# Moving one weight block's decode behind a second set of peaks, and spreading four pairs' sums by transposes

## The chip, the cores and the metric

The kernel runs on one core of one Trainium2 chip. The metric is the device time of one execution in microseconds (us). The engines are named as the profile names them: PE is TensorE's matmul, PEld its weight load, DVE is VectorE, ACT is ScalarE, POOL is GpSimd and SP is SyncE, which issues most of the DMAs. A small letter q behind an engine (SPq, ACTq) is that engine's queue of DMA issues.

## What is computed

Attention with a window of 128 keys and 4 sink keys, and a feed-forward network on what comes out of it. The shapes are B=4, H=8, S=768 and D=64 for q, k and v, and 3072 tokens with 512 to 2048 to 512 features for the network; `w_in` and `w_out` come as 64-bit floats.

```python
keep = is_sink | in_window                      # S x S
scores = np.where(keep, scores, -1000000000.0)
scores = scores - np.max(scores, axis=-1, keepdims=True)
a = np.exp(scores)
a = a / (np.sum(a, axis=-1, keepdims=True) + 1e-09)
attn_out = np.matmul(a, v)

x = attn_out.transpose(0, 2, 1, 3).reshape(B * S, H * D)
h = x @ w_in
g = np.where(h >= 1, h, np.where(h <= -1, 0.0, (h + 1) ** 2 / 4))
return g @ w_out
```

## The kernel before, in words

The 3072 tokens are cut into eight chunks of 384, a chunk being one batch entry and one half of its sequence. For each chunk the attention of eight heads fills `xn`, 512 features by 384 tokens, `split` (L617) turns that into two halves `x`, a rounded part and the rest, and the network runs on them: `stage1` (L582, its matmuls at L588) and `stage2` (L602, matmuls at L607), three matmuls for each product. The attention of chunk c+1 is spread over the network of chunk c, so PE always has network matmuls to do, except ahead of the first chunk: there `first_pairs` (L523) does the attention of chunk 0 with nothing to cover it.

The first sixteen heads (chunks 0 and 1) are computed in plain float32, two heads at a time, in eight **pairs** m = 0 to 7. For one pair:

- `pair_load` (L408) fetches keys and queries (DMAs at L415 and L416), `pair_values` (L419) the values `vq` (L423, L424);
- `pair_scores` (L431) does two score matmuls for each of three row tiles (L441), into `o_ps`, `h_ps` or `ps_a`; DVE takes the row maxima, called **peaks** below (L452), and ACT the exponentials with their row sums (L457);
- `pair_sums` (L460) adds 1e-9 (L464) and takes the reciprocals (L465): six numbers for each partition;
- `early_transp` (L468) transposes the weights of the two heads on PE (L474, L476), and ACT copies them to `pt` (L477, L478, L480);
- `pair_r` (L498) spreads the reciprocals: six float32 matmuls (L505), each of 64 by 128 outputs, whose left operand is one column of reciprocals broadcast to 64 columns and whose right operand is the identity. ACT copies the 128 by 384 result to `xn` (L507);
- `pair_av` (L482) multiplies weights and values (L493), and DVE multiplies `xn` by the product (L496).

Pairs 0 to 3 and the scores of pair 4 are in `first_pairs`. Pairs 5 to 7 and what is left of pair 4 are written as steps with weights (`pair_steps`, L509) and spread over the network of chunk 0: `spread` (L637) takes attention steps so that their summed weights keep pace with those of the network's steps, so a step's weight sets where PE does it.

The weights come in sixteen blocks of 1 MB, `w_in` and `w_out` in turn, and must be **decoded** from 64-bit words before use. One decode is four steps (L164 on): shift on DVE (L170), sign on DVE (L176), tail on DVE (L179) with a copy on ACT (L180), and the rest on DVE (L183); each of the DVE steps is on 128 by 1024 elements. Blocks 0 to 3 are decoded inside `first_pairs`, a step here and there between the pairs' peaks; there `d[0]` to `d[3]` are the four steps, in `m`'s turn. The other twelve are spread over chunk 0's network. The block's DMA (L205) is issued by SP for blocks 0 to 3 and by ACT for the others.

What sets the order: PE works in program order. In `first_pairs`, DVE and ACT instructions that go through `queue` (L64) are also kept in program order among themselves. Every other instruction of DVE, ACT, POOL and SP is placed by the compiler's scheduler, which plans each engine's queue from a model of the whole program; an engine then works through its queue strictly in that order. Loads for the first head of chunk 2, whose attention follows the pairs (`load`, L262 and L264, and `values`, L324, with its cast to `vsx` at L326 on ACT and the subtract at L327 on POOL), have no need of anything before them and are placed inside `first_pairs`' stretch. The tile `vs_r` has one buffer, so each L324 waits until POOL's L327 of the one before is done.

Of the kernel before, what the change touches and what calls it, by code (L numbers as in the profile page):

```python
# [8 lines left out]
F32 = mybir.dt.float32  # L9
F32R = mybir.dt.float32r  # L10
# [5 lines left out]
B, H, S, D = 4, 8, 768, 64  # L16
DM, DFF = 512, 2048
P = 128
NT = S // P
CT = 3  # L20
# [29 lines left out]
def attn_ffn(ctx, tc, qk, qkp, vx, vs, par, w_in, w_out, out):  # L50
    nc = tc.nc
# [12 lines left out]
    def queue(i, on=True):  # L64
        if on:
            e = i.ins.engine
            if e in queued:
                tc.add_manual_dep(i.ins, queued[e].name, mybir.DependencyInfo(
                    mybir.DependencyClass.NoSync, mybir.DependencyReason.DATA), reason="queue")
            queued[e] = i.ins  # L70
        return i

    ident = const.tile([P, P], F32, name="ident")
# [176 lines left out]
    att = fast.enter_context(tc.tile_pool(name="att", bufs=2))  # L250
    fast.enter_context(tc.manual_schedule(engines={mybir.EngineType.PE}))
    st = {}
# [155 lines left out]
    def pair_load(m):  # L408

        b, h, _ = units[2 * m]  # L410
        T = CT * P
        W = CT * KB - NSINK
        q_s = att.tile([P, T], F32R, name="q_h").bitcast(F32)
        k_s = att.tile([P, P + CT * KB], F32R, name="k_s").bitcast(F32)[:, :W]
        loaded.append(nc.sync.dma_start(k_s, qkp[b, h // 2, :, T:T + W]).ins)  # L415
        nc.sync.dma_start(q_s, qkp[b, h // 2, :, 0:T])  # L416
        st["qk", m] = q_s, k_s

    def pair_values(m):  # L419
        v_s = vq[m % 2]  # L420
        for a in range(2):
            b, h, _ = units[2 * m + a]
            nc.sync.dma_start(v_s[:, :CT, a], vx[b, h, :, :CT])  # L423
            nc.sync.dma_start(v_s[:NSINK, CT, a], vx[b, h, :NSINK, 0])  # L424
# [35 lines left out]
    def pair_sums(m):  # L460
        on = m < H // 2
        stat = st.pop(("sum", m))
        r = stat[:, :, CT:2 * CT]
        queue(nc.vector.tensor_scalar(r, stat[:, :, 0:CT], 1.0e-9, None, op0=ALU.add), on)  # L464
        queue(nc.vector.reciprocal(r, r), on)  # L465
        st["r", m] = r

    def early_transp(u, part):  # L468

        p, pt = early_p(u), pt0[u % 2]  # L470
        on = u < H
        ps = ps_a.tile([P, 512], F32, name="ps_a")
        for n, (i, c) in enumerate((((0, KB), (1, 0), (1, KB)), ((2, 0), (2, KB)))[part]):
            nc.tensor.transpose(ps[:, n * P:(n + 1) * P], p[:, i, c:c + P], ident)  # L474
        if part:
            nc.tensor.transpose(ps[:NSINK, 2 * P:CT * P], p[:, CT - 1, P:KB], ident)  # L476
            queue(nc.scalar.copy(pt[:, CT * P:5 * P], ps[:, :2 * P]), on)  # L477
            queue(nc.scalar.copy(spn[u % 2][:NSINK], ps[:NSINK, 2 * P:CT * P]), on)  # L478
        else:
            queue(nc.scalar.copy(pt[:, :CT * P], ps[:, :CT * P]), on)  # L480

    def pair_av(m):  # L482

        T = CT * P
        v_s = vq[m % 2]
        ps = ps_a.tile([P, 512], F32, name="ps_a")

        terms = [(2, 4, 1, 2), (0, 0, 2, 0), (1, 2, 2, 1), None]
        for n, t in enumerate(terms):
            for a in range(2):  # L490
                k, s0, ns, i = t or (CT, 0, 1, CT - 1)
                rhs = pt0[a][:, s0 * P:(s0 + ns) * P] if t else spn[a]
                nc.tensor.matmul(ps[a * D:a * D + D, i * P:(i + ns) * P], lhsT=v_s[:, k, a], rhs=rhs,  # L493
                                 start=(n == 0), stop=(n == len(terms) - 1))
        x = xn[:, units[2 * m][1] // 2, :]
        return lambda: queue(nc.vector.tensor_tensor(x, ps[:, :T], x, op=ALU.mult), m < H // 2)  # L496

    def pair_r(m):  # L498

        T = CT * P  # L500
        ps = ps_a.tile([P, 512], F32, name="ps_a")
        r = st.pop(("r", m))
        for i in range(CT):
            for a in range(2):
                nc.tensor.matmul(ps[a * D:a * D + D, i * P:(i + 1) * P], lhsT=r[:, a, i:i + 1].broadcast_to([P, D]),  # L505
                                 rhs=ident, start=True, stop=True)
        queue(nc.scalar.copy(xn[:, units[2 * m][1] // 2, :], ps[:, :T]), m < H // 2)  # L507

    def pair_steps(m):  # L509

        a, b = 2 * m - 2, 2 * m - 1
        sc = [(0.45, lambda i=i: pair_scores(m, i)) for i in range(CT)] if m < NATIVE // 2 else [(0.0, lambda: None)] * CT
        steps = [(0.0, lambda: pair_load(m + 1))] if m + 1 < NATIVE // 2 else []
        if m < NATIVE // 2:
            steps.append((0.0, lambda: pair_values(m)))
        tp = [(0.35, lambda u=u, i=i: early_transp(u, i)) for u in (a, b) for i in range(2)]
        pv = [(0.65, lambda: pair_r(m - 1)), (1.2, lambda: pair_av(m - 1)())]
        dg = [(0.0, lambda: pair_sums(m))] if m < NATIVE // 2 else []
        if m % (H // 2) == 0:
            return steps + tp[:3] + sc[:1] + tp[3:] + pv[:1] + sc[1:2] + pv[1:] + sc[2:] + dg  # L520
        return steps + tp[:1] + sc[:1] + tp[1:] + sc[1:2] + pv + sc[2:] + dg

    def first_pairs():  # L523
        pair_load(0)
        pair_load(1)
        pair_values(0)
        d = None
        for m in range(H // 2 + 1):
            if m:
                pair_load(m + 1)  # L530
                pair_values(m)
                for u in (2 * m - 2, 2 * m - 1):
                    for part in range(2):
                        early_transp(u, part)
            if m == H // 2:
                pair_r(m - 1)
                d[2]()
                pair_av(m - 1)()
            pair_scores(m, 0)
            pair_scores(m, 1)  # L540
            if 0 < m < H // 2:
                d[2]()
            pair_scores(m, 2)
            if m:
                d[3]()
            if 0 < m < H // 2:
                pair_r(m - 1)
            pair_sums(m)
            if m < H // 2:
                wsteps[m][0]()  # L550
                d = wsteps[m][1]()
                d[0]()
                if m:
                    pair_av(m - 1)()
                d[1]()


    chunks = [(b, t) for t in (0, CT) for b in range(B)]
# [101 lines left out]
    wsteps = [weights(n) for n in range(NP)]  # L660
# [33 lines left out]
    ps = ps_a.tile([P, 512], F32, name="ps_a")  # L694
# [56 lines left out]
    with tc.If(other_v > 0):  # L751
        with tc.tile_pool(name="gen", bufs=1) as gen:

            for n in range(2 * NJ):
# [3 lines left out]
                m = gen.tile([P, DM], F32, name="m")  # L758
# [3 lines left out]
            for t0 in (0, CT):  # L762
                keep = gen.tile([P, CT, S], F32, name="keep")
                kidx = gen.tile([P, S], I32, name="kidx")
                r = gen.tile([P, S], F32, name="r")
                for i in range(CT):
                    m = keep[:, i]
# [54 lines left out]
```

## Time and profile before

| what | value |
|---|---|
| runs | 706.54 us, median of 3 (705.92 to 707.37) |
| profiled execution, own time | 705.98 us |
| its span in the profile | 704.3 us |
| mean granted TensorE clock | 0.994 of full speed |
| busy: PE, DVE, ACT, POOL | 681.5, 510.3, 489.5, 278.8 us |
| instructions | 12263 |

The span runs from the first instruction's start to the last one's end; 1.7 us of the execution's time lie around it. Busy times include time in which an instruction stands in the engine's pipeline, so two neighbours can overlap by some tenths of a microsecond. In the timeline a row gives the start, the time of one or of several merged instructions, the engine, the line of the kernel, and the operation with the tile written, an arrow and the tiles read; in square brackets stands how long the engine was idle before, and what ended that.

### The profile page before, as it was taken

How to read it: one execution, taken by the hardware profiler on the slowest of the kernel's cores; microseconds unless marked ns; L12 is line 12 of the kernel's file. 1: busy time of each engine (PE TensorE's matmuls, PEld its weight loads, DVE VectorE, ACT ScalarE, POOL GpSimd, SP SyncE). 2: the span in 40 equal slices, each digit the busy share in tenths (PEclk: the TensorE clock that was granted, in tenths of full speed). 3: DMA queues.
4: the chain of work that ended last, by engine and by line, in shares of the span. 5: the costliest groups of instructions: out<-in, count | busy, mean ns of one | idle time of the engine just before them, and what ended most of it. 6: DMA issues, size and time to landing. Idle time of an engine off the chain costs nothing.

```text
span 704.3 us, 12263 instructions
## 1 busy us (share of the span) xinstructions
PE 681.5 (97%) x3889; PEld 604.6 (86%) x3889; DVE 510.3 (72%) x1405; ACT 489.5 (70%) x1241; POOL 278.8 (40%) x470
## 2 busy tenths in 40 slices
PE   5899998999999999999999999999999999999996
PEld 3567877899999999989889999899899999989995
DVE  7888998887776877688777878878787877642221
ACT  4886667687778868777787877777776876554332
POOL 3003344744443445355554455635544444300000
PEclk9899999999999999999999999999999999999999
DMA  7864533132244344254333443434322310001001
GB/s 232 291 216 156 190 99 135 49 107 60 63 148 124 102 127 129 68 174 128 92 113 105 147 130 124 126 118 133 122 59 62 102 50 22 3 1 45 1 1 49
DMA packets 45441, 73.98 MB, mean 105 GB/s; under 512 B 10744, under 2 KB 30008, under 8 KB 45368
## 3 DMA queue, kind: packets, MB, share of 16 engines
q1 hardware_dynamic: 42104, 60.53, 28.2%
q10 hardware_dynamic: 3264, 12.58, 4.8%
q8 instruction: 33, 0.54, 0.3%
q14 instruction: 40, 0.33, 0.1%
HBM read 66.80 MB, written 6.29 MB: 104 GB/s over the span
## 4 chain that ended last, share of the span: by engine, by line
PE 79%; DVE 9%; DMA 3%; ACT 3%; POOL 3%; issue 2%; SPq 0%; ACTq 0%; POOLq 0%; DVEq 0%
PE h_ps L588 33%; PE o_ps L607 32%; PE ps_a L283 4%; PE ps_a L390 4%; PE ps_a L344 2%; DVE bits L176 2%; DVE bits L179 1%; DMA w<-w_in 1%; POOL q_l L269 1%; PE ps_a L474 1%; DVE w L183 1%; DVE bits L170 1%; PE ps_a L493 1%; DVE p L304 1%; DVE g L597 1%
## 5 line engine op out<-in xcount | busy, mean ns | idle before, releaser
L588 PE MATMUL h_ps<-x,wi 128*128 128x384 f32 x1536 | 310.2, 340 | 0.0
L588 PEld LDWEIGHTS h_ps<-x,wi 128*128 128x128 f32 x1536 | 262.2, 188 | 8.7 <-issue 1.5
L607 PE MATMUL o_ps<-w,gh 128*128 128x512 f32 x768 | 244.0, 398 | 0.0
L607 PE MATMUL o_ps<-w,gl 128*128 128x512 f32 x384 | 151.1, 393 | 0.4 <-POOL gl L599 0.4
L607 PEld LDWEIGHTS o_ps<-w,gh 128*128 128x128 f32 x768 | 134.3, 188 | 16.9 <-issue 1.7
L597 DVE SCALAR_TENSOR_TENSOR g<-g,h_ps 128x384 f32<-128x384 f32 x128 | 70.3, 549 | 61.7 <-ACT g L596 60.6
L595 ACT ACTIVATE g<-h_ps,half 128x384 f32<-128x384 f32 x128 | 73.9, 578 | 52.7 <-PE h_ps L588 52.0
L269 POOL TENSOR_TENSOR q_l<-r,q_h 128x384 fp32r<-128x384 f32 x48 | 51.1, 1064 | 122.7 <-ACT q_h L268 116.1
L598 ACT CAST gh<-g 128x384 fp32r<-128x384 f32 x128 | 65.5, 512 | 46.1 <-DVE g L597 44.9
L290 ACT ACTIVATE p<-p,peak 128x260 f32<-128x260 f32 (+1 forms) x144 | 71.5, 496 | 23.0 <-DVE peak L287 22.4
L607 PEld LDWEIGHTS o_ps<-w,gl 128*128 128x128 f32 x384 | 72.0, 188 | 17.8 <-POOL gl L599 0.7
L599 DVE TENSOR_TENSOR gl<-g,gh 128x384 fp32r<-128x384 f32 x112 | 67.3, 601 | 23.5 <-ACT gh L598 22.6
L267 DVE TENSOR_TENSOR k_s<-k_r,k_s 64x524 fp32r<-64x524 f32 (+1 forms) x44 | 49.1, 1115 | 34.4 <-ACT k_s L265 34.3
L596 ACT ACTIVATE g<-g 128x384 f32<-128x384 f32 x128 | 67.0, 524 | 2.0
L287 DVE CUSTOM_DVE_ANT_0 p<-ps_a,m 128x260 f32<-128x260 f32 (+1 forms) x144 | 57.0, 407 | 14.7 <-PE ps_a L283 13.8
L358 POOL TENSOR_SCALAR_AFFINE_SELECT pt<-pt 128x384 fp32r<-128x384 f32 (+1 forms) x96 | 51.3, 535 | 22.6 <-DVE pt L349 19.5
L304 DVE CUSTOM_DVE_ANT_0 p<-p,stat 128x128 f32<-128x128 f32 x128 | 57.0, 489 | 0.2
L356 POOL TENSOR_SCALAR_AFFINE_SELECT pt<-pt 128x384 fp32r<-128x384 f32 (+1 forms) x96 | 49.9, 521 | 8.8 <-ACT pt L348 4.9
L599 POOL TENSOR_TENSOR gl<-g,gh 128x384 fp32r<-128x384 f32 x16 | 23.4, 1461 | 67.7 <-ACT gh L598 64.2
L390 PEld LDWEIGHTS ps_a<-pt,v_s 128*128 128x128 f32 x304 | 42.4, 190 | 1.8
L390 PE MATMUL ps_a<-pt,v_s 128*128 128x256 f32 (+1 forms) x304 | 41.9, 275 | 0.0
L283 PE MATMUL ps_a<-k_s,q_h 128*128 128x260 f32 (+1 forms) x144 | 40.7, 283 | 1.2 <-DVE sk L352 0.9
(151 smaller groups left out, 933.1 us busy)
## 6 DMA issues: line engine op xcount, KB each, us to landing
r<-qk SPq DMA_DIRECT2D x48, 192.0 KB
k_r<-qk SPq DMA_DIRECT2D x32, 262.0 KB
again<-w_in SPq DMA_DIRECT2D x16, 512.0 KB
again<-w_out SPq DMA_DIRECT2D x16, 512.0 KB
w<-w_in ACTq DMA_DIRECT2D x6, 1024.0 KB
w<-w_out ACTq DMA_DIRECT2D x6, 1024.0 KB
out<-o SPq DMA_DIRECT2D x23, 256.0 KB
r<-vx SPq DMA_DIRECT2D x32, 128.0 KB
```

What stands on the lines that cost most here:

```text
L269: nc.gpsimd.tensor_tensor(q_l, q_r, q_h.bitcast(F32), op=ALU.subtract)
L283: nc.tensor.matmul(ps[:, lo:260], lhsT=q[:, i * P:(i + 1) * P], rhs=k_s[:, c0:c0 + 260 - lo], start=(j == 0), stop=(j == len(qs) - 1))
L290: nc.scalar.activation(p[:, i, lo:260], p[:, i, lo:260], AF.Exp, bias=peak_i, scale=-1.0, accum_out=stat[:, i:i + 1])
L304: nc.vector.tensor_tensor_reduce(out=own, in0=own, in1=p[:, i, 0:P], scale=r, scalar=0.0, op0=ALU.add, op1=ALU.add, accum_out=stat[:, i:i ...
L390: nc.tensor.matmul(z, lhsT=w, rhs=y, start=(n == 0), stop=(n == len(mms) - 1))
L588: nc.tensor.matmul(h_ps[:, :T], lhsT=w_i[j][:, w, ct * P:(ct + 1) * P], rhs=x[:, y, ct], start=(ct == 0 and n == 0), stop=(ct == NCT - 1 a ...
L595: nc.scalar.activation(g, h_ps[:, :T], AF.Relu, bias=half, scale=0.5)
L596: nc.scalar.activation(g, g, AF.Square)
L597: nc.vector.scalar_tensor_tensor(g, g, 1.0, h_ps[:, :T], op0=ALU.min, op1=ALU.max)
L598: nc.scalar.copy(gh, g)
L599: (nc.gpsimd if row0 == GL_POOL else nc.vector).tensor_tensor(gl, g, gh.bitcast(F32), op=ALU.subtract)
L607: nc.tensor.matmul(o_ps[tt], lhsT=gg[:, tt * P:(tt + 1) * P], rhs=w_o[j][:, w], start=(j == 0 and n == 0), stop=(j == NJ - 1 and n == 2))
```

## The change

Two edits, the first in `first_pairs`, the second in `pair_sums`, `pair_r` and `pair_steps`.

1. **Block 0.** In turn m=0 only the fetch of block 0 is left. All its four decode steps now stand in turn m=1, behind the six peaks of pair 1 and ahead of pair 1's sums. Before, shift and sign stood behind pair 0's sums, the tail between the fourth and the fifth peak of pair 1, and the rest behind the sixth. Blocks 1 to 3 keep their places.
2. **Pairs 4 to 7.** The reciprocal is no longer taken of six numbers in place. One reciprocal reads each of the six numbers 64 times (a broadcast read) and writes 128 by 384 numbers into a tile called `q_l`, a name that `load` also uses, with two buffers. `pair_r` then needs three transposes of 128 by 128, one for each row tile, in place of six broadcast matmuls. For m > 4 the weight of that step falls from 0.65 to 0.35.

```diff
@@ -462,8 +462,13 @@
         stat = st.pop(("sum", m))
         r = stat[:, :, CT:2 * CT]
         queue(nc.vector.tensor_scalar(r, stat[:, :, 0:CT], 1.0e-9, None, op0=ALU.add), on)
-        queue(nc.vector.reciprocal(r, r), on)
-        st["r", m] = r
+        if on:
+            queue(nc.vector.reciprocal(r, r))
+            st["r", m] = r
+        else:
+            wide = st["r", m] = att.tile([P, CT * P], F32R, name="q_l").bitcast(F32).rearrange(
+                "p (i a d) -> p i a d", a=2, d=D)
+            nc.vector.reciprocal(wide, r.rearrange("p a i -> p i a").unsqueeze(3).broadcast_to([P, CT, 2, D]))
 
@@ -501,6 +506,9 @@
         for i in range(CT):
+            if m >= H // 2:
+                nc.tensor.transpose(ps[:, i * P:(i + 1) * P], r[:, i].rearrange("p a d -> p (a d)"), ident)
+                continue
             for a in range(2):
@@ -514,7 +522,7 @@
-        pv = [(0.65, lambda: pair_r(m - 1)), (1.2, lambda: pair_av(m - 1)())]
+        pv = [(0.35 if m > H // 2 else 0.65, lambda: pair_r(m - 1)), (1.2, lambda: pair_av(m - 1)())]
@@ -538,21 +546,24 @@
                 pair_av(m - 1)()
             pair_scores(m, 0)
             pair_scores(m, 1)
-            if 0 < m < H // 2:
+            if 1 < m < H // 2:
                 d[2]()
             pair_scores(m, 2)
-            if m:
+            if m == 1:
+                for f in wsteps[0][1]():
+                    f()
+            elif m:
                 d[3]()
             if 0 < m < H // 2:
                 pair_r(m - 1)
             pair_sums(m)
             if m < H // 2:
                 wsteps[m][0]()
-                d = wsteps[m][1]()
-                d[0]()
                 if m:
+                    d = wsteps[m][1]()
+                    d[0]()
                     pair_av(m - 1)()
-                d[1]()
+                    d[1]()
```

On DVE, in `first_pairs`, around the peaks of pair 1 (L452, `pt,peak`): a piece of the difference between the two orders. `wi_155` is block 0's place, `bits` the words being decoded.

```order
-L179 SCALAR_TENSOR_TENSOR bits_232<-w,bits_232 128x1024
 L452 ISA pt,peak<-h_ps,m_106 128x260
 L452 ISA peak 128x1
 L452 ISA pt,peak<-ps_a,m_106 128x260
 L452 ISA peak 128x1
-L183 TENSOR_TENSOR wi_155<-bits_232,wi_155 128x2x512
+L170 TENSOR_SCALAR bits_287<-w 128x1024
+L176 SCALAR_TENSOR_TENSOR bits_287<-w,bits_287 128x1024
+L179 SCALAR_TENSOR_TENSOR bits_287<-w,bits_287 128x1024
+L183 TENSOR_TENSOR wi_155<-bits_287,wi_155 128x2x512
 L464 TENSOR_SCALAR stat<-stat 128x2x3
```

Block 0's steps have left the place ahead of and between the peaks, and stand in a row behind the last of them.

On ACT, just after pair 1's exponentials, up to those of pair 2 (L457, `p,stat`): the order of the change. `vsx` is the cast of `vs_r` for chunk 2; L515, L485, L482 and L629 are what L507, L480, L477 and L618 were before.

```order
L180 CAST wi_155<-bits_287 128x2x512
L515 COPY xn<-ps_a 128x384
L485 COPY pt<-ps_a 128x384
L326 CAST vsx_149<-vs_r 120x128
L482 COPY pt<-ps_a 128x256
L483 COPY spn_179<-ps_a 4x128
L485 COPY pt<-ps_a 128x384
L482 COPY pt<-ps_a 128x256
L483 COPY spn_180<-ps_a 4x128
L629 CAST x<-xn 128x384
L326 CAST vsx_150<-vs_r 120x128
L457 ACTIVATE p,stat<-p,peak 128x128 x2
```

Before, the first of these casts of `vs_r` stood behind all of pair 1's copies to `pt`, and the second behind four of pair 2's exponentials.

On SP, in the same stretch: a piece of the difference. The DMA `w<-w_out` at L205 is block 3, whose decode is the last in `first_pairs`.

```order
-L324 DMA vs_r<-vs 120x128
-L415 DMA k_s<-qkp 128x392
-L416 DMA q_h<-qkp 128x384
+L324 DMA vs_r<-vs 120x128 x2
+L415 DMA k_s<-qkp 128x392
+L416 DMA q_h<-qkp 128x384
+L423 DMA vq_178<-vx 128x3x64
 L205 DMA w<-w_out 128x2x1024
-L324 DMA vs_r<-vs 120x128
-L423 DMA vq_178<-vx 128x3x64
```

Block 3's load has now a third load of `vs_r` and one of `vq` ahead of it, which stood behind it.

## Rows read from the trace of the kernel before

**Rows 1.** The page's chain that ended last: share of the span by engine.

```profile
PE 79%; DVE 9%; DMA 3%; ACT 3%; POOL 3%; issue 2%; SPq 0%; ACTq 0%; POOLq 0%; DVEq 0%
```

**Rows 2.** Busy time by engine in five stretches: first_pairs, then chunk 0's network.

```profile
core 0: us, PE busy (x) PEld busy (x) DVE busy (x) ACT busy (x) POOL busy (x), PEclk, DMA share, GB/s
0.00:42.70 42.70, 30.21 (x223) 20.83 (x224) 35.18 (x118) 29.62 (x94) 6.50 (x36) 0.92 0.78 255
42.70:60.00 17.30, 17.30 (x110) 13.95 (x109) 14.71 (x26) 12.50 (x34) 4.25 (x3) 1.00 0.48 171
60.00:80.00 20.00, 20.00 (x122) 15.68 (x121) 17.45 (x31) 12.72 (x32) 4.85 (x3) 1.00 0.59 209
80.00:100.00 20.00, 20.00 (x124) 15.52 (x123) 19.86 (x32) 13.19 (x34) 8.29 (x6) 1.00 0.39 126
100.00:120.00 20.00, 19.78 (x126) 16.84 (x125) 17.73 (x28) 13.39 (x32) 9.94 (x7) 1.00 0.27 93
```

**Rows 3.** Timeline of DVE: block 0's decode, pair 1's first peak, block 3's shift.

```profile
12.88 0.70 DVE L170 TENSOR_SCALAR bits<-w 128x1024 int32<-128x1024 int32 x1 [2.91 <-DMA w<-w_in]
13.62 1.23 DVE L176 SCALAR_TENSOR_TENSOR bits<-w,bits 128x1024 int32<-128x1024 int32 x1
14.76 0.28 DVE L452 CUSTOM_DVE_ANT_0 pt<-o_ps,m 128x128 f32<-128x128 f32 x1
...
15.88 1.22 DVE L179 SCALAR_TENSOR_TENSOR bits<-w,bits 128x1024 int32<-128x1024 int32 x1
...
18.21 1.23 DVE L183 TENSOR_TENSOR wi<-bits,wi 128x1024 fp32r<-128x1024 f32 x1 [0.42 <-ACT wi L180]
...
35.71 0.65 DVE L170 TENSOR_SCALAR bits<-w 128x1024 int32<-128x1024 int32 x1
```

**Rows 4.** Timeline of ACT: block 0's copy, pair 1's copies, the casts of vs_r.

```profile
17.13 1.05 ACT L180 CAST wi<-bits 128x1024 fp32r<-128x1024 f32 x1 [0.17 <-DVE bits L179]
...
19.08 0.45 ACT L507 COPY xn<-ps_a 128x384 f32<-128x384 f32 x1
...
20.27 0.37 ACT L477 COPY pt<-ps_a 128x256 f32<-128x256 f32 x1 [0.36 <-PE ps_a L476]
...
22.27 0.29 ACT L326 CAST vsx<-vs_r 120x128 fp32r<-120x128 f32 x1
...
25.20 0.28 ACT L326 CAST vsx<-vs_r 120x128 fp32r<-120x128 f32 x1
```

**Rows 5.** Line L324 on SP up to 60 us: its issues and the semaphore waits.

```profile
L324 SPq EVENT_SEMAPHORE  x2: 28/28/28, 21.4 to 25.3; - x2
```

**Rows 6.** Timeline of SP: second vs_r, block 3, keys behind it.

```profile
23.18 0.34 SPq L324 DMA_DIRECT2D vs_r<-vs  x1
...
24.80 0.43 SPq L205 DMA_DIRECT2D w<-w_out  x1
...
34.33 0.34 SPq L415 DMA_DIRECT2D k_s<-qkp  x1
```

**Rows 7.** Waits of SP's queue from 4 to 44 us: in total, times, longest.

```profile
SPq L415 <- DMA w<-w_out: 5.0, 1, 5.0
```

**Rows 8.** Timeline of PE: one pair_r, and one group of three transposes.

```profile
91.44 0.88 PE L505 MATMUL ps_a<-ident,stat 128*64 128x128 f32 x12
92.25 0.96 PE L588 MATMUL h_ps<-x,wi 128*128 128x384 f32 x4
...
101.80 0.49 PE L474 MATMUL ps_a<-ident,pt 128*128 128x128 f32 x3
102.05 0.71 PE L607 MATMUL o_ps<-w,gh 128*128 128x512 f32 x2
```

**Rows 9.** Groups by line and shape: the reciprocals (count; busy us, mean ns; idle before).

```profile
L296 DVE RECIPROCAL stat<-stat 128x3 f32<-128x3 f32 x48 | 8.4, 175 | 9.4 <-POOL stat L295 7.1
L465 DVE RECIPROCAL stat<-stat 128x6 f32<-128x6 f32 x8 | 1.5, 190 | 0.2
```

**Rows 10.** Timeline of DVE and PE: block 10's last step, and its first use.

```profile
92.70 2.04 DVE L183 TENSOR_TENSOR wi<-bits,wi 128x1024 fp32r<-128x1024 f32 x1
...
98.17 1.04 PE L588 MATMUL h_ps<-x,wi 128*128 128x384 f32 x5
```

## The prediction

> **What bounds the kernel now.** I read the chain that ended last first: PE holds 79% of it and DVE 9% [rows 1]. So most of the span is a row of matmuls, and what counts is how late that row begins and what stands in it that needn't. The busy times by stretch say where DVE's share lies [rows 2]. In the first 42.7 us, which are `first_pairs`, PE is busy 30.21 us and DVE 35.18: there the pairs' peaks, the decode of four blocks and ACT's copies hand work to each other, and PE waits. From 42.7 on PE is busy in every microsecond up to 100. A microsecond gained or lost before 42.7 therefore moves the end of the kernel by as much; after that a microsecond of PE work taken out is gained in full, as long as DVE, busy 19.86 of 20 us between 80 and 100, doesn't fall behind with the blocks that PE needs.
>
> The rest was read engine by engine for two questions: who waits around block 0's decode [rows 3, 4], and what SP has ahead of the load of block 3 [rows 6].
>
> **Edit 1, block 0.** Before, DVE stands idle for 2.91 us until block 0 has landed at 12.88, with pair 1's peaks queued behind shift and sign; the first peak starts at 14.76, the tail stands between the peaks, and the last step starts at 18.21 [rows 3]. The change puts the six peaks first. They need nothing of block 0. Four of them are done between the rows at 14.76 and 15.88, in 1.1 us, and the last two, longer ones, take about 0.7 (my estimate from that spacing). PE's score matmuls feed them one after another, so I put their end near 13.9. Shift, sign and tail then follow without a break: 0.74 and 1.14 us by the starts at 12.88, 13.62 and 14.76, and some 1.15 for the tail, together 3.0, so the tail ends at 16.9, against 17.1 before. ACT's copy of 1.05 us [rows 4] ends at 18.0, and the last step starts at 18.1 against 18.21. For DVE's own queue the edit is worth 0.1 us: four steps on end cost what the idle time gave.
>
> What does come earlier is ACT's part. Its six exponentials no longer straddle block 0's copy; behind that copy stands at once the copy to `xn` (L507), which moves from 19.08 [rows 4] to about 18.1, 1.0 us earlier. If that ran through to the end of the stretch, edit 1 would give 1.0 us. That is its lower end, -1.0.
>
> Two things take it back, and both are in the new orders. First, ACT now has the cast of `vs_r` (L326) between pair 1's first and second copy to `pt`. The data of that cast land at 21.4, where SP's wait for it ends [rows 5]; before, the cast stood behind all those copies, at 22.27, and waited for nothing. Now ACT waits from about 18.5 to 21.4, and pair 1's second copy, at 20.27 before [rows 4], comes at 21.4 + 0.29 = 21.7, 1.4 us later. Behind it on ACT stand the three other copies, the split of `x` and pair 2's exponentials; PE waits for those copies to have its PSUM buffers back. The 1.0 us lead is lost here.
>
> Second, SP's queue. The second load of `vs_r` was issued at 23.18, 0.9 us after the cast at 22.27 (POOL's subtract must free the buffer), and its cast came at 25.20, 2.0 us after the issue [rows 4, 6]. With the first cast at 21.4, the second load goes at 22.3, its cast at 24.3, the third load at 25.2. Keys, queries and a load of `vq` follow, at some 0.42 us each by the issue times of these rows, and block 3 is issued at 26.9 instead of 24.80, **2.1 us later**. SP had to wait 5.0 us for that very block before its next issue at 34.33 [rows 6, 7], so it landed at 34.3, and DVE's shift of it ran at 35.71 [rows 3]: the slack is 1.4 us. With the same time to land it comes at 36.4, and the shift waits 0.7 us. DVE keeps its order, so `xn`'s product, the split of `x`, the peaks of pair 4 and so the first network matmul are queued behind this wait. I take **+0.7** for edit 1. Its upper end: if another 1 MB load goes first through the DMA engines at the stretch's 255 GB/s [rows 2], the block lands 4.1 us later still, and edit 1 costs 4.8.
>
> **Edit 2, on PE.** One `pair_r` holds PE from 91.44 to 92.25, 0.81 us, and three transposes of 128 by 128 from 101.80 to 102.05, 0.25 us [rows 8]. The new three are of the same shape, so each of the four pairs gives 0.56 us, 2.2 in all. ACT's copy behind it stays. The lower step weight moves neighbouring attention steps by a few network matmuls; PE has the same work in another order, and I cost that at nothing, since network matmuls cover it up to 100 us. POOL's first `q_l` must wait for one of the two buffers until a pair's transposes are done; its reader, the first head of chunk 2, is scored some 10 us after that, so nothing here either.
>
> **Edit 2, on DVE.** The trace has no reciprocal of 128 by 384. 128 by 3 takes 175 ns, 128 by 6 takes 190 [rows 9]: 5 ns for each further number, which gives 0.19 + 378 x 0.005 = 2.1 us; I take it since these are the only reciprocals there are. It can't be below the 0.19 us of six numbers. Upward, if all of the 190 ns went with the numbers, it would be 12.2 us, but then half the numbers would take 95 ns and not 175. Two means that lie 15 ns apart, of two shapes, can be off: I let the slope be wrong by 70% either way, 0.8 to 3.4 us, and keep these as the ends. The four wide ones add 4 x (2.1 - 0.19) = 7.6 us to DVE. The Trainium skill's page "VectorE: DVE Perf Modes", section "Walkthrough: the 8-slice pipeline in each mode", says that a reciprocal is an iterated divide with a repeat count of 8; at the 0.96 GHz of the same page that would be 8.3 ns for each number where the rows show 5, an estimate of 3.4 us for the wide one, and the sum would be that of the second rival below.
>
> DVE's idle time from 42.7 to 120 is 2.59 + 2.55 + 0.14 + 2.27 = 7.55 us [rows 2], so the added 7.6 just fill it, but not where it is needed. The first two wide ones fall into stretches with over 2.5 us to spare and are hidden. The third falls between 80 and 100, with 0.14 to spare; its overrun of 1.8 meets the fourth's stretch, where 2.27 - 1.9 = 0.4 is left, and 1.4 us remain. They eat into the slack of the decoded blocks (block 10 is finished at 94.74 and used at 98.17, 3.4 us [rows 10]), and DVE must still feed PE behind. So I count two of the four savings: **-1.1**.
>
> **The sum.** +0.7 - 1.1 = -0.4 us. Against the profiled execution's own 705.98 that is 705.6; this execution lay 0.56 below the median of the runs, so against 706.54 I predict **706.1**. What a measurement can tell from no change is about 0.2%, 1.4 us: no change is 705.1 to 708.0.
>
> **The rivals.**
>
> Faster: the load of block 3 has time enough (for it: it has 1.4 us of slack, and a load issued later may meet emptier queues; against it: DMA is 0.78 busy in this stretch [rows 2]), the 1.0 us lead of `xn` runs through, and DVE hides all four reciprocals in the decode slack. Then -1.0 - 2.2, 703.3.
>
> Slower, by the reciprocal: if it takes 3.4 us, the four add 12.8 to DVE; 7.55 of idle and 3.4 of block 10's slack cover 10.95, PE waits 1.9, no saving of PE is left, and edit 1 adds 0.7: 709.1. It decides from 2.9 us on, where 4 x (x - 0.19) passes 10.95. For it speaks that two shapes of 3 and 6 numbers are a thin base for 384; against it the slope they show. The page named above is the rule that would bring it; by these rows, the trace doesn't agree with its 8.
>
> Slower, by the load: block 3 lands behind a further 1 MB, edit 1 costs 4.8, and 706.54 + 4.8 - 1.1 is 710.2. It decides once the block lands later than 38.2, 2.5 us past the old shift (706.54 + 2.5 - 1.1 = 707.9). Against it: nothing else of that size moves ahead of it on SP.
>
> **How the numbers follow.** My forecast has a chance of 0.44, the faster rival 0.28, the reciprocal 0.17, the load 0.11. So faster by over 0.2% is 0.28, within it 0.44, slower 0.28. The range is 703.2 to 710.0: below it lies the faster rival with the decode slack used up as well, above it the late load in full and a reciprocal beyond 3.4 us, under 0.2 together. The forecast's own range is 705.1 to 708.0.
>
> **What would show it.** In the profile after: pair 1's peaks done by about 14 and block 0's shift starting behind them; ACT idle ahead of the cast of `vs_r` until about 21.4; SP's issue of block 3 near 26.9 and DVE waiting for it at its last shift; the first network matmul about 0.7 us after 42.7. The wide reciprocal shows its length by itself: near 2.1 us the forecast stands, near 0.8 the faster case gains, over 2.9 the slower. DVE's stretch from 80 to 100 should hold no idle time, and PE should gain 0.56 us at each pair. I am wrong if DVE's last shift in `first_pairs` doesn't wait, or if PE shows waits on decoded blocks after 85.

## The result, and the profile after

The changed kernel takes 715.33 us, median of 4 runs (713.28 to 716.99), against 706.27 for the kernel before in the same comparison (705.92 to 707.37). The ratio is 1.0124, 95% interval 1.0092 to 1.0157: **slower, by 6.5 to 11.1 us**. The prediction was 706.1 with a range of 703.2 to 710.0. It was wrong. The profiled execution took 714.27 us, with a span of 712.5.

Busy time by stretch, as in [rows 2], with one stretch more:

```profile
core 0: us, PE busy (x) PEld busy (x) DVE busy (x) ACT busy (x) POOL busy (x), PEclk, DMA share, GB/s
0.00:42.70 42.70, 29.41 (x216) 20.30 (x218) 33.07 (x105) 27.92 (x86) 6.49 (x36) 0.92 0.76 249
42.70:60.00 17.30, 16.35 (x105) 13.33 (x102) 16.67 (x37) 12.93 (x38) 3.08 (x2) 1.00 0.42 146
60.00:80.00 20.00, 19.34 (x111) 15.29 (x110) 19.29 (x29) 12.16 (x33) 5.98 (x4) 1.00 0.53 193
80.00:100.00 20.00, 19.95 (x115) 15.52 (x113) 19.79 (x30) 14.19 (x35) 6.51 (x4) 1.00 0.45 153
100.00:120.00 20.00, 17.11 (x100) 13.91 (x100) 20.00 (x22) 10.80 (x25) 9.60 (x6) 1.00 0.30 96
120.00:140.00 20.00, 15.81 (x82) 13.31 (x81) 18.69 (x40) 12.95 (x33) 14.63 (x14) 1.00 0.29 93
```

From 60 on DVE hardly rests, and between 100 and 120 it is busy in every microsecond, while PE, which was busy for 19.78 there [rows 2], has 17.11. Before, PE led and DVE followed; here it is the other way round in the second half of chunk 0's network.

The profiled execution's span is 8.2 us longer than before's. Chunk 1's network begins 5.63 us later than before, 141.97 in place of 136.34:

```profile
136.34 0.68 PE L588 MATMUL h_ps<-x,wi 128*128 128x384 f32 x3
```

```profile
141.97 0.68 PE L599 MATMUL h_ps<-x,wi 128*128 128x384 f32 x3
```

From there to the end this execution takes 570.5 us and before's 567.9. The experiments' profiles below take 568.5 to 570.2 there, and 569.9 one whose only edit holds some early loads back (e6). So before's was the quickest of them all, and how much of these last 2.6 us belongs to the edits can't be told.

Up to chunk 1 the time goes in two places. The first is the start of the network, 44.95 in place of 42.72. DVE around block 0, pair by pair up to the last product of `first_pairs`, to be held against [rows 3]:

```profile
12.10 0.29 DVE L452 CUSTOM_DVE_ANT_0 pt<-o_ps,m 128x128 f32<-128x128 f32 x1 [1.97 <-PE o_ps L441]
...
12.96 0.43 DVE L452 CUSTOM_DVE_ANT_0 pt<-o_ps,m1n 128x260 f32<-128x260 f32 x1 [0.36 <-PE h_ps L441]
...
14.53 0.69 DVE L170 TENSOR_SCALAR bits<-w 128x1024 int32<-128x1024 int32 x1
...
18.85 1.23 DVE L183 TENSOR_TENSOR wi<-bits,wi 128x1024 fp32r<-128x1024 f32 x1 [1.11 <-ACT wi L180]
...
36.19 0.65 DVE L170 TENSOR_SCALAR bits<-w 128x1024 int32<-128x1024 int32 x1
...
42.32 0.56 DVE L501 TENSOR_TENSOR xn<-ps_a,xn 128x384 f32<-128x384 f32 x1 [2.28 <-PE ps_a L498]
```

DVE is idle again, now for PE's scores, and block 0's last step starts at 18.85, later than the 18.21 of [rows 3]. Block 3's shift at 36.19 waits for nothing. The 2.28 us in the last row are the largest loss: DVE waits for PE's products of pair 3. Before, the same wait was 0.32:

```profile
39.89 0.56 DVE L496 TENSOR_TENSOR xn<-ps_a,xn 128x384 f32<-128x384 f32 x1 [0.32 <-PE ps_a L493]
```

On PE the products of the kernel after are the second row here:

```profile
38.33 1.30 PE L513 MATMUL ps_a<-ident,stat 128*64 128x128 f32 x12
39.41 2.35 PE L498 MATMUL ps_a<-pt,vq 128*64 128x128 f32 x12
...
44.95 0.77 PE L599 MATMUL h_ps<-x,wi 128*128 128x384 f32 x3
```

In the kernel before the same twelve matmuls took 1.52 us:

```profile
38.05 1.52 PE L493 MATMUL ps_a<-pt,vq 128*64 128x128 f32 x12
```

The stretch of the slow ones in the kernel after shows why; the sixth figure after the stretch's length, PEclk, is the granted clock, 0.50 of full speed, so it is at TensorE's lower level, 1.2 and not 2.4 GHz:

```profile
38.60:42.00 3.40, 3.40 (x28) 2.44 (x24) 1.44 (x2) 1.92 (x5) 0.00 (x0) 0.50 0.25 29
```

The kernel before was granted no more of the full clock in these 42.7 us: 0.92 in both. Its lower clock lay elsewhere, from 20.0 to 23.4 and from 30.2 to 33.6, and not over these products. Before the clock fell at 38.6, PE had waited 1.14 and 0.69 us, for ACT's copy and for DVE's product:

```profile
36.13 0.44 PE L479 MATMUL ps_a<-ident,pt 128*128 128x128 f32 x2 [1.14 <-ACT xn L515]
...
37.36 0.77 PE L479 MATMUL ps_a<-ident,pt 128*128 128x128 f32 x5 [0.69 <-DVE xn L501]
```

The second of these waits comes from a new place on ACT. The split of `x` now stands ahead of three copies of transposed weights, and ACT waits there for DVE's product:

```profile
37.34 0.51 ACT L629 CAST x<-xn 128x384 fp32r<-128x384 f32 x1 [0.89 <-DVE xn L501]
```

Before, it stood behind those three copies and waited for nothing; the first of them and the split:

```profile
36.29 0.37 ACT L477 COPY pt<-ps_a 128x256 f32<-128x256 f32 x1 [0.32 <-PE ps_a L476]
...
37.09 0.51 ACT L618 CAST x<-xn 128x384 fp32r<-128x384 f32 x1
```

The second place is chunk 0's network. These are PE's waits there of half a microsecond or more; before, the 1.94 us that the last of them answers to, at 122.89, was the only one:

```profile
66.03 0.48 PE L441 MATMUL ps_a<-k_s,q_h 64*128 64x128 f32 x2 [0.66 <-DVE peak L452]
112.10 0.52 PE L510 MATMUL ps_a<-ident,q_l 128*128 128x128 f32 x3 [2.75 <-DVE q_l L471]
112.38 0.71 PE L618 MATMUL o_ps<-w,gh 128*128 128x512 f32 x2
...
124.91 0.39 PE L283 MATMUL ps_a<-k_s,q_h 128*128 128x260 f32 x1 [2.06 <-DVE peak L287]
...
128.87 0.87 PE L344 MATMUL ps_a<-ident,p 128*128 128x128 f32 x3 [1.81 <-DVE p L302]
```

They add up to 7.28 us, 5.3 more than before. Less some 2.1 us that the transposes save on PE, that is near the 3.4 us by which the delay grows from the start of chunk 0's network to that of chunk 1's.

And the group of the wide reciprocals (count; busy us, mean ns; idle before):

```profile
L471 DVE RECIPROCAL q_l<-stat 128x384 f32<-128x384 f32 x4 | 10.2, 2550 | 0.1
```

### The profile page after: what moved, and what is told of

Its sections match the earlier page's. It is cut to its first block, busy times and chain, and to the rows that moved or that the text cites. A ratio compares the mean times of both kernels' runs of the same rounds, so it can differ in the third digit from the quotient of the medians.

```text
span 712.5 us, 12195 instructions
## 1 busy us (share of the span) xinstructions
PE 680.6 (96%) x3853; PEld 603.4 (85%) x3853; DVE 520.9 (73%) x1405; ACT 488.6 (69%) x1241; POOL 278.7 (39%) x470
## 5 line engine op out<-in xcount | busy, mean ns | idle before, releaser
L618 PE MATMUL o_ps<-w,gh 128*128 128x512 f32 x768 | 243.6, 398 | 0.0
L618 PE MATMUL o_ps<-w,gl 128*128 128x512 f32 x384 | 151.1, 393 | 0.3 <-POOL gl L610 0.3
L618 PEld LDWEIGHTS o_ps<-w,gh 128*128 128x128 f32 x768 | 134.3, 189 | 15.3 <-issue 0.7
L618 PEld LDWEIGHTS o_ps<-w,gl 128*128 128x128 f32 x384 | 72.0, 188 | 17.7 <-POOL gl L610 0.7
```

The lines of the kernel that those rows point to most:

```text
L618: nc.tensor.matmul(o_ps[tt], lhsT=gg[:, tt * P:(tt + 1) * P], rhs=w_o[j][:, w], start=(j == 0 and n == 0), stop=(j == NJ - 1 and n == 2))
```

## The experiments

In each comparison below, us are what the measured ratio exceeds 1 by, times 706 (the ratio can differ by 0.001 from the quotient of the medians); every kernel is compared with the kernel before on its own chip. Theory 1 is what the profile after suggested: edit 1 delays the start of the network, edit 2 overloads DVE, and the two add up.

**e1: edit 1 alone.** Of the diff of the change, the part in `first_pairs`; `pair_sums`, `pair_r` and `pair_steps` are as before.

> Block 0's decode moved as in the change, pairs 4 to 7 as before. The profile of the changed kernel shows the first network matmul 2.2 us late, with the half clock granted over pair 3's last products. Theory 1 (the two edits cost separately): this kernel is 2 to 3 us slower than before, 708 to 709.5, its first network matmul is near 44.9, and PE shows no wait over 1 us on DVE between 100 and 128. Rival (the late start only eats into slack that is there later): within 0.7 us of before. Rival (edit 1 sets off everything, since a late start meets DVE's decode deadlines): 6 us or more slower.

Measured: 1.0073 (1.0045 to 1.0102), +5.2 us. More than expected. The profiled execution, the slowest of the five with 714.77 us, shows what I had forecast and the profile after didn't have: ACT waiting for `vs_r` and DVE for block 3.

```profile
22.11 0.30 ACT L326 CAST vsx<-vs_r 120x128 fp32r<-120x128 f32 x1 [2.69 <-DMA vs_r<-vs]
```

```profile
39.99 0.69 DVE L170 TENSOR_SCALAR bits<-w 128x1024 int32<-128x1024 int32 x1 [2.01 <-DMA w<-w_out]
```

Its network starts at 49.05, 6.3 us later than before's. In the profile after, `vs_r` had landed by 19.7 and block 3, issued at 25.08, was there in time. The queues are the same in this stretch, the loads are not equally fast from one execution to the next. So that mechanism is real and strikes some executions; how many, these profiles don't tell. It isn't needed for the scatter of the changed kernel (3.7 us over 4 runs): the kernel before, on e1's chip, scatters over 5.7 us in 21 runs.

**e2: edit 2 alone. e4: four wide reciprocals that nobody reads.** e2 is the rest of that diff: `first_pairs` is as before. e4 is the kernel before with this added to `pair_sums`; it computes what the kernel before does:

```diff
+        if not on:
+            wide = att.tile([P, CT * P], F32R, name="q_l").bitcast(F32).rearrange("p (i a d) -> p i a d", a=2, d=D)
+            nc.vector.reciprocal(wide, r.rearrange("p a i -> p i a").unsqueeze(3).broadcast_to([P, CT, 2, D]))
         queue(nc.vector.reciprocal(r, r), on)
```

> Pairs 4 to 7 as in the change (one wide reciprocal, three transposes), block 0's decode as before. Theory 1: the first network matmul is at 42.7 as before, the wide reciprocals take 2.55 us each, 9.4 us more on DVE, which has 7.55 us of idle time there; PE waits 4 to 5 us on DVE between 100 and 130 and saves 2 on the spread: 2 to 4 us slower than before, 708.5 to 710.5. Rival (the late start of edit 1 is needed for DVE to fall behind): within 0.7 us of before or faster. Rival (edit 2 is all of it): 7 us or more slower.

> The kernel before, with four wide reciprocals added whose results nothing reads; the narrow reciprocals and the six broadcast matmuls stay. Theory 1: DVE's 10.2 us more make PE wait as in the changed kernel and no PE work goes, so about 2.2 us slower than the kernel with wide reciprocals and transposes: 4 to 6.5 us slower than before. Rival (the cost lies in PE waiting for the spread itself, not in DVE's load): within 1 us of before, since nothing waits for these results.

Measured: e2 1.0063 (1.0044 to 1.0081), +4.4 us; e4 1.0099 (1.0067 to 1.0130), +7.0 us. Both somewhat more than expected, and in the expected order. Nothing reads e4's wide tiles, yet PE waits, for a block's last decode step and for a small reciprocal queued behind:

```profile
100.08 0.97 PE L591 MATMUL h_ps<-x,wi 128*128 128x384 f32 x4 [1.17 <-DVE wi L183]
...
111.29 0.88 PE L508 MATMUL ps_a<-ident,stat 128*64 128x128 f32 x12 [2.15 <-DVE stat L468]
```

So DVE's load alone costs; PE need not read the wide tile for it. The 2.6 us between e4 and e2 are near what the transposes save on PE, which I had put at 2.2; as the two intervals overlap, the size isn't sure. With e1, the two edits alone add up to 9.6 us, the change measured 8.8.

**e3 and e7: the spread without the division.** Reciprocal of six numbers as before, then a plain copy that writes each 64 times, on ACT (e3, the diff below) or on DVE (e7, with `nc.vector.tensor_copy` in its place), then the three transposes; block 0 as before.

```diff
-            nc.vector.reciprocal(wide, r.rearrange("p a i -> p i a").unsqueeze(3).broadcast_to([P, CT, 2, D]))
+            nc.vector.reciprocal(r, r)
+            nc.scalar.copy(wide, r.rearrange("p a i -> p i a").unsqueeze(3).broadcast_to([P, CT, 2, D]))
```

> As the one before, but the reciprocal is of six numbers again, and ACT copies them 64 times each into the wide tile; PE does the three transposes. DVE gets no more work than before. Theory 1 (DVE's time in the wide reciprocal is what edit 2 costs): 1.5 to 2.5 us faster than before, 704 to 705, since four times 0.56 us of PE work go and ACT has room for four copies of about 0.5 us. Rival (the transposes or the tile shared with the loads bring the cost, by waits of POOL and PE): as slow as the kernel with the wide reciprocal.

> Block 0 as before; pairs 4 to 7 with a reciprocal of six numbers, a plain copy on DVE that writes each of them 64 times, and the three transposes. Theory 1 (the division repeated 384 times is what DVE pays for): the copy takes 0.3 to 0.6 us, DVE has 1.2 to 2.4 us more work in place of 9.4, and the time lies within 1 us of the kernel with the copy on ACT, 705 to 707. Rival (writing or reading 128 by 384 numbers by a broadcast is slow whatever the operation): the copy takes 2 us or more and the time is 710 or more.

Measured: e3 0.9988 (0.9969 to 1.0006), -0.8 us; e7 0.9992 (0.9975 to 1.0009), -0.6 us. The groups of the two copies:

```profile
L472 DVE COPY q_l<-stat 128x384 f32<-128x384 f32 x4 | 2.2, 550 | 0.1
```

```profile
L472 ACT COPY q_l<-stat 128x384 f32<-128x384 f32 x4 | 2.0, 503 | 0.0
```

Writing 128 by 384 numbers from a broadcast read takes 550 ns on DVE, the division 2550. Without the division the loss of edit 2 is gone. So is the rival that the transposes, or the tile name shared with the loads, bring it: both are in e3 and e7. But e3's expected gain of 1.5 to 2.5 us is missed: PE's saving of some 2.1 us doesn't arrive in full at the end. In e3's profile PE waits again, later:

```profile
114.42 0.30 PE L283 MATMUL ps_a<-k_s,q_h 128*128 128x128 f32 x1 [0.86 <-DVE peak L287]
...
119.83 0.87 PE L344 MATMUL ps_a<-ident,p 128*128 128x128 f32 x3 [2.31 <-DVE p L302]
```

These are the first scores and transposes of chunk 2, which hang on a chain of DVE, ACT and POOL work; PE comes to them earlier and waits longer (3.17 us in the two, 1.94 before). Then the lower clock is granted from 121.1 to 124.5; but it is granted at that place in e9 and e12 below too (122.5 to 125.9, 121.2 to 124.6), which keep the six broadcast matmuls, so it needs no new spread. This is one reading of one profile, and no run separates it. That part of the saving is lost is measured, by e3 and e7 together (each interval alone reaches to about -2 us); how it is lost is argued.

**e11: two wide, two copied.** Pairs 4 and 5 with the wide reciprocal, 6 and 7 with e7's copy; block 0 as before.

```diff
-            nc.vector.reciprocal(wide, r.rearrange("p a i -> p i a").unsqueeze(3).broadcast_to([P, CT, 2, D]))
+            six = r.rearrange("p a i -> p i a").unsqueeze(3).broadcast_to([P, CT, 2, D])
+            if m < 6:
+                nc.vector.reciprocal(wide, six)
+            else:
+                nc.vector.reciprocal(r, r)
+                nc.vector.tensor_copy(wide, six)
```

> Block 0 as before; pairs 4 and 5 with the wide reciprocal, pairs 6 and 7 with the reciprocal of six and a copy on DVE; transposes for all four. All four wide ones cost 4.5 us, none with the copy on DVE 0. Theory 1 (the first two wide ones fall into DVE's idle time and only the last two make PE wait): within 1 us of before. Rival (each one pushes the decode back and the delay is carried on, so every one costs its part): 2 to 3 us slower than before.

Measured: 1.0009 (0.9989 to 1.0029), +0.6 us, against +4.4 for four wide ones. Within the interval, which reaches to 2.0, the first two are hidden in DVE's idle time, as the prediction had it; the third and the fourth bring most of the 4.4.

**e5 and e6: the loads of vs_r held back**, with edit 1 (e5) and with the kernel before (e6).

```diff
-            nc.sync.dma_start(vs_r, vs[b, h // 2])
+            with tc.issue_after(loaded[-1]) if units.index(u) < NATIVE + 6 else nullcontext():
+                nc.sync.dma_start(vs_r, vs[b, h // 2])
```

> Block 0's decode moved as in the change, pairs 4 to 7 as before, and the loads of vs_r held back behind the keys of pair 7, so that neither their issues on SP nor their casts on ACT stand in the first 43 us any more. Block 0's move alone cost 5.6 us. Theory 1 (the casts of vs_r, waited for by ACT ahead of pair 1's copies, and block 3's load, late behind vs_r on SP, bring most of it): 1 to 3 us slower than before, and in the profile neither ACT waits for vs_r nor DVE for block 3. Rival (the half clock after PE's longer waits, or the four decode steps on end, bring it): still 4 us or more slower.

> The kernel before with the loads of vs_r held back in the same way: the control of the last one. Theory 1: before, these casts wait for nothing and stand behind the copies, so within 0.7 us of before. Rival (holding the loads back costs or gains by itself): over 1 us either way, and then the last one must be read against this.

Measured: e5 1.0055 (1.0037 to 1.0074), +3.9 us; e6 1.0003 (0.9982 to 1.0025), +0.2. The rival holds: without any wait for `vs_r` or block 3, most of edit 1's cost stays. Of the 5.2 us, 1.3 go with these loads, and with intervals that overlap even that is not certain. The pair tells more than either alone, since no load of `vs_r` stands ahead of the network in either. Block 0's steps on DVE in e5, then in e6:

```profile
14.41 0.69 DVE L170 TENSOR_SCALAR bits<-w 128x1024 int32<-128x1024 int32 x1
...
18.73 1.23 DVE L183 TENSOR_TENSOR wi<-bits,wi 128x1024 fp32r<-128x1024 f32 x1 [1.11 <-ACT wi L180]
```

```profile
11.49 0.69 DVE L170 TENSOR_SCALAR bits<-w 128x1024 int32<-128x1024 int32 x1 [1.52 <-DMA w<-w_in]
...
16.81 1.23 DVE L183 TENSOR_TENSOR wi<-bits,wi 128x1024 fp32r<-128x1024 f32 x1 [0.42 <-ACT wi L180]
```

In e6 block 0 is there at 11.49, not at the 12.88 of [rows 3], and its shift and sign run while PE still makes pair 1's scores. The last step starts 1.92 us earlier than in e5 (0.69 of it is the shorter wait for ACT's copy), and this difference stays in DVE's queue to block 3's shift (35.88 and 33.97). Then e5 loses 1.7 more: in e5 the split of `x` has its new place on ACT, in e6 the old one, and most of the 1.7 are lost over pair 3's spread and products, at the lower clock (from 38.4 to 41.8). It starts its network at 44.55, e6 at 40.95:

```profile
44.55 0.78 PE L592 MATMUL h_ps<-x,wi 128*128 128x384 f32 x3
```

```profile
40.95 0.77 PE L589 MATMUL h_ps<-x,wi 128*128 128x384 f32 x3
```

**e9: only the tail and the rest behind the peaks.** Shift and sign stay ahead of pair 1's peaks.

```diff
-            if 0 < m < H // 2:
+            if 1 < m < H // 2:
                 d[2]()
             pair_scores(m, 2)
+            if m == 1:
+                d[2]()
             if m:
                 d[3]()
```

> Block 0's shift and sign ahead of pair 1's peaks as before, and only its tail and its rest behind all six peaks. Theory 1 (edit 1 costs because DVE idles while PE makes pair 1's scores, and then does all four steps on end: 1.9 us between the two kernels with vs_r held back): shift and sign use that idle time again, so at most 1 us slower than before, 705.5 to 707. Rival (taking the decode out of the peaks costs in itself, by ACT's copy that then stands behind all exponentials): 3 us or more slower.

Measured: 1.0001 (0.9979 to 1.0024), no difference. The shift runs at 11.88 and the last step at 17.91, though ACT's copy stands behind all exponentials here too:

```profile
11.88 0.69 DVE L170 TENSOR_SCALAR bits<-w 128x1024 int32<-128x1024 int32 x1 [1.92 <-DMA w<-w_in]
...
17.91 1.23 DVE L183 TENSOR_TENSOR wi<-bits,wi 128x1024 fp32r<-128x1024 f32 x1 [1.12 <-ACT wi L180]
```

So what costs in edit 1 is that shift and sign leave the time in which DVE has nothing else to do. In this profile and the experiments' eight others that keep shift and sign ahead of pair 1's peaks, the network starts at 40.46 to 41.80, always earlier than the 42.72 of the profile before, so the 2.23 us between the profiles before and after tell too little of edit 1.

**e10 and e12: PE's waits filled.** e5 and e6 with transposes of the identity, which nothing reads, ahead of a pair's first and second group of transposes; their numbers by pair differ.

```diff
+                f = ps_o.tile([P, 512], F32, name="o_ps")
                 for u in (2 * m - 2, 2 * m - 1):
                     for part in range(2):
+                        for _ in range(FILL[m][part] if u % 2 == 0 else 0):
+                            nc.tensor.transpose(f[:, 0:P], ident, ident)
                         early_transp(u, part)
```

> Block 0's decode moved, vs_r held back (that kernel was 3.9 us slower than before), and transposes of the identity, which nothing reads, added on PE where it waits between pairs: 20, 23 and 9 of them. Theory 1 (of those 3.9 us some 1.4 to 2 are the half clock that PE is granted after these waits): no half clock in the profile between 15 and 45 us, the first network matmul at 42.5 to 43.2 in place of 44.55, and 1.4 to 2.5 us slower than before. Rival (the clock falls for another reason, or its fall is hidden): the half clock stays, or the time stays at 3.5 us or more above before.

> The kernel before with vs_r held back, and transposes of the identity on PE where it waits between pairs (21, 9 and 15): a version that might beat the kernel before. Theory 1 (PE's waits bring the half clock): none of it between 15 and 43 us, the first network matmul at 40.9 or a little earlier in every execution, 0.5 to 1.5 us faster than the same kernel without them, 704.5 to 705.5. Rival (these transposes delay the chain where they meet real work): no faster, 706 to 707.5.

Measured: e10 1.0032 (1.0012 to 1.0053), +2.3 us, where e5 had +3.9; e12 0.9978 (0.9956 to 0.9999), -1.6 us, the fastest of all, just clear of no change. Granted clock from 15 us, or from 16 in e12, to the start of the network: e5, e10, e6, e12.

```profile
15.00:44.50 29.50, 21.01 (x174) 13.99 (x169) 24.75 (x64) 20.73 (x63) 0.00 (x0) 0.88 0.73 251
```

```profile
15.00:41.70 26.70, 22.60 (x214) 17.02 (x211) 24.52 (x64) 20.24 (x63) 0.00 (x0) 1.00 0.77 257
```

```profile
16.00:40.90 24.90, 18.30 (x158) 12.49 (x159) 22.71 (x66) 20.85 (x65) 0.00 (x0) 0.93 0.79 267
```

```profile
16.00:40.70 24.70, 21.86 (x213) 16.60 (x208) 23.23 (x68) 20.95 (x66) 0.00 (x0) 1.00 0.83 273
```

With the fill the full clock holds, 0.88 and 0.93 become 1.00. e10 starts its network at 41.75, 2.8 us earlier than e5; 1.4 to 2.0 of that were expected of the clock. The scheduler also put the split of `x` back to its old place on ACT in e10, which has its part: 1.5 of the 2.8 us are there at PE's last spread (36.51 and 38.02), ahead of e5's fall at 38.4. But the lower clock then came at 43.0, over the first network matmuls, where nine take 3.13 us that took 1.83 in e5, and the gain at the end is 1.6:

```profile
42.87 3.13 PE L597 MATMUL h_ps<-x,wi 128*128 128x384 f32 x9
```

The expectation that no half clock would be granted up to 45 was thus missed by 2.0 us. The network of e10 starts as early as that of e9 (41.71), and yet e10 is 2.2 us slower: what is left of its cost comes behind the start. The intervals of e5 and e10 overlap, as do those of e6 and e12, so the gains of 1.6 and 1.8 us are not better known.

They are alike, and that matters: with the fill in both kernels, edit 1 still costs 3.8 us (e10 less e12), without it 3.7 (e5 less e6). The fill gains the same whether block 0 is moved or not, so it doesn't show that edit 1 costs by the clock. Nor do waits like those of the profile after always bring the lower clock. In e6 PE waits 0.71 and 1.14 us, 1.65 us apart as against 1.23 there, and from then on to the start of the network the full clock is granted:

```profile
32.26 0.52 PE L475 MATMUL ps_a<-ident,pt 128*128 128x128 f32 x3 [0.71 <-DVE peak L453]
33.91 0.44 PE L475 MATMUL ps_a<-ident,pt 128*128 128x128 f32 x2 [1.14 <-ACT xn L508]
```

```profile
34.00:41.00 7.00, 5.59 (x53) 3.96 (x53) 6.72 (x20) 5.58 (x17) 0.00 (x0) 1.00 0.72 208
```

**e8: the ACT spread with vs_r held back**, a candidate: the edits of e3 and of e6 together.

> Block 0 as before, the spread copied by ACT, and the loads of vs_r held back: a version that might beat the kernel before. If holding back changes nothing and the spread on ACT gives its 0.4 us, 705.5 to 706.7. If the casts of vs_r delay some executions of the kernel before as well, up to 2 us faster, 704 to 705.

Measured: 1.0038 (1.0019 to 1.0057), +2.7 us: a miss. Its network starts early, at 40.46, and PE then waits 2.5 us on DVE and ACT between 82 and 93, which neither e3 nor e6 does. From the start of the network to 112 us DVE has the same work in the same order as in e3, and runs up to 0.5 us ahead of it, until one wait. ACT waits for the second of the loads held back, and DVE for ACT's `g` behind it:

```profile
71.31 0.30 ACT L327 CAST vsx<-vs_r 120x128 fp32r<-120x128 f32 x1 [3.48 <-DMA vs_r<-vs]
```

```profile
72.14 0.55 DVE L607 SCALAR_TENSOR_TENSOR g<-g,h_ps 128x384 f32<-128x384 f32 x1 [3.20 <-ACT g L606]
```

In e3 the same step of DVE starts at 69.22 without a wait, and from there e8's DVE is 2.6 to 3.0 us behind e3's up to 112. In e6 the same cast waits 1.12 us. So in the profiled execution a load that the edit took out of the start of the kernel is waited for inside chunk 0's network. That this is the 2.7 us of all runs is likely, but no run separates it.

## Why the prediction was wrong, by its own steps

**"For DVE's own queue the edit is worth 0.1 us: four steps on end cost what the idle time gave."** This is the step that failed first. It erred twice. The peaks were put at an end near 13.9; they are paced by PE's scores and end at 14.53, with idle time between them. And the 2.91 us of idle time [rows 3] were taken as the kernel's, when they were that execution's: in the nine other profiles in which shift and sign stand ahead of the peaks, block 0's shift starts at 11.04 to 12.20. In those, the decode uses the idle time. Taking it away costs 1.9 us in DVE's queue (e5 against e6), and leaving it shift and sign takes edit 1's cost away (e9, 0.1 us with an interval up to 1.7). The prediction's own sign of being wrong showed: the last shift in `first_pairs`, at 36.19, doesn't wait.

**"I take +0.7 for edit 1", bounds -1.0 to +4.8.** Measured alone +5.2 (3.2 to 7.2). The two mechanisms named, the cast ahead of the copies and block 3's later issue, did occur as described in e1's profiled execution, with 2.69 and 2.01 us. In that of the change itself neither did: the casts wait 0.30 at most, block 3 not at all. Held back, 1.3 of 5.2 us went. What the sum had at nothing is what lies between e5 and e6: the 1.9 us above, and 1.7 behind them, where the split of `x` stands at a new place on ACT and the lower clock falls on pair 3's spread and products. How these 1.7 are shared between the two is open. The row with 0.92 for this stretch [rows 2] stood in front of me, and I priced nothing with it; but the share of full clock is 0.92 after too, and the fill gains as much without edit 1. The first paragraph's rule, that a microsecond before 42.7 moves the end by as much, holds only roughly: e6's profile starts its network 1.77 us earlier than before's, and its span is 0.7 longer.

**"5 ns for each further number, 2.1 us."** It was 2.55, so (2550 - 190) / 378 = 6.2 ns. Within the ends of 0.8 to 3.4, the slope mis-sized by a quarter. The Trainium skill's page "VectorE: DVE Perf Modes", section "Walkthrough: the 8-slice pipeline in each mode", gives a repeat count of 8; at the page's 0.96 GHz that is an estimate of 8.3 ns for each number. The trace doesn't agree with it: the measured 6.2 ns lies between that and my 5, and decides.

**"So I count two of the four savings: -1.1."** The account of idle time was right in kind: e11 shows the first two hidden, within its interval, and so most of the cost in the last two. Its end was wrong. At 2.55 us the four add 9.4 us to 7.55 of idle time, and the remainder was let off against the slack of block 10 [rows 10]. But blocks aren't the only thing PE takes from DVE: it waited 2.75 us for the fourth reciprocal itself and 2.06 for a peak of chunk 2, both queued behind decode steps that came late. Edit 2 costs 4.4 alone where -1.1 was forecast. The rival put its turning point at 2.9 us for one reciprocal; by e2 it lies below 2.55.

**"Each of the four pairs gives 0.56 us, 2.2 in all."** Right as PE's time: the spread takes 0.28 us (112.10 to 112.38), so each pair gives 0.53. As a gain at the end it didn't come in full: e3 and e7, which have it without the load on DVE, gain 0.8 and 0.6 us, and neither is clear of no change.

## What to carry to other kernels

A gap in one trace is that execution's gap: before pricing what is moved out of it, ask what ends it and whether another execution would end it sooner, above all when a load does. An engine that is busy 19.86 of 20 us in a stretch has no room for a second-order cost, and slack must be counted for everything that is read from it, not for its largest product alone. A load that is held back is waited for somewhere else: look for its reader's new place before calling the edit free. In a stretch that nothing covers, it also matters where the lower clock falls: before and after had the same share of it, and only after had it on the products that end the chain.

## What the runs showed of the hardware

A float32 reciprocal of 128 by 384 takes DVE 2550 ns, 6.2 ns for each number past the six that take 190 ns; a copy of the same shape takes 550 ns. Waits of PE don't settle by themselves whether the granted clock falls: 1.14 and 0.69 us preceded the fall at 38.6 in the profile after, 0.71 and 1.14 were followed by none in e6, and 2.75, 2.06 and 1.81 us between 110 and 129 by none in the profile after. With 52 transposes of the identity in such waits it stayed at 1.00 from 15 to 41.7 us in e10. The kernel before scattered from 703.1 to 710.2 us over 85 runs on three chips, much more than the 705.9 to 707.4 that the first runs showed.
